# Attention output of some token groups by seven block products for pairs of tiles

## The chip, the cores and the metric

The kernel runs on one core of one Trainium2 chip. The metric is the device time of one execution in microseconds (us). The time before is the median of three runs, 1319.13 us (1318.87 to 1319.29).

## What is computed

Two layers with the same weights, each a linear-attention block followed by a feed-forward block with squared ReLU, on 2048 tokens of width 640 (32 heads of 20), in fp32:

```python
x = A_x
x = x + _A_ref(_layernorm(x), A_wqkv, A_wo)
x = x + _B_ref(_layernorm(x), B_w1, B_b1, B_w2, B_b2)
# the same two lines once more

# _A_ref: q, k, v = x @ wqkv; pq, pk = phi(q), phi(k)
kv = jnp.einsum("bhsd,bhse->bhde", pk, v)
z = jnp.einsum("bhsd->bhd", pk)
num = jnp.einsum("bhqd,bhde->bhqe", pq, kv)
den = jnp.einsum("bhqd,bhd->bhq", pq, z)[..., None] + 1e-6
return (num / den).reshape(B, S, D) @ wo
# _B_ref: h = relu(x @ w1 + b1) ** 2; return h @ w2 + b2      (F = 1728)
```

## The kernel before, in words

**Tiles and exact products.** The 2048 tokens are 16 tiles of 128 rows; four tiles make a group (`TG`, groups 0 to 3). Every fp32 operand of a matmul is split into a high and a low part (`split`: ScalarE copies the rounded high part, VectorE subtracts to get the low part), and each product is three matmuls: high by low, low by high, high by high.

**A layer.** First the attention sums over all tokens are formed. Since kv is the same for all tokens, kv and `wo` are multiplied together once per layer into one 640 by 640 matrix. It is kept split in SBUF as five tiles `M[0]` to `M[4]` of 128 rows (`uM` in the profile). The attention output of a tile is then its normalized pq, transposed, times M: 5 row blocks x 2 column halves of 320 x 3 matmuls = 30 matmuls of 128x320.

**The feed-forward block** runs over the four groups. For each group, `fc1` takes 14 steps c (15 matmuls of 128x512 each, 10 in the last); `act` follows each on ScalarE (Relu, Square) and writes to the tile `R`. Then come 28 steps n of `fc2_step` (12 matmuls of 128x320, or fewer), which already multiply by seven block products with sums and differences formed by `s_op`; `u_hi` (ScalarE) and `u_lo` (VectorE) split them into the five slots of the tile `arena`. The results are added to the residual tile `xr[t]` by `fc2_add`.

**Work beside it.** While group g goes through the feed-forward block, the attention output of the four tiles of group g + 1 is computed (`single`). For a tile t: `b_load_pq` loads pq; `b_den` forms the denominator in a tile `pr`; `b_blocks` divides and transposes 32x32 blocks into a tile `y`; `blocks_move` puts the blocks in place with 16 small ScalarE copies (32x160) into `z`; `p_split` splits into `pTs`; `out` issues the 30 matmuls, in PSUM banks 6 and 7, right after `fc1` steps 4, 7, 10 and 13 (`OUTS`); `add` adds them to `xr[t]` and takes the layernorm's sums; `store` normalizes and writes to DRAM; later `spread_in` and `x_split` bring the tile into `xTb`, the input of the next group's `fc1`.

**Order.** Nothing is scheduled by a tool: each engine runs its instructions in the order in which the code emits them, and `at(g, c, f)` and `on(n, f)` put f after step c of group g (n below zero means the end of the group before, n from 14 on means its `fc2` part, two steps to one). After step c the order is: `fc1` matmuls on TensorE, `load_ring`, `act`, the ("pe", c) events, the other events of c in the order of their registration.

**Weights.** They do not fit in SBUF. `Units` streams them from DRAM copies (`kept`) through a ring of six buffers `u`; a unit's load is issued by SyncE (SP), in order with all other loads and stores, when the matmuls of the unit six places earlier are done. `load_stay` loads the units of `fc2` that stay (`uw`), one per step from c = 3 of group 0. In layer 0, group 0 also runs the last part of the weight preparation (`prep_last`).

Of the kernel before, what the change touches and what calls it, by code (L numbers as in the profile page):

```python
# [13 lines left out]
P = 128  # L14
# [37 lines left out]
AHEAD = 2  # L52
F_BUFS, X_BUFS = 8, 5
OUTS = (4, 7, 10, 13)


def unit_range(k):
# [8 lines left out]
def kernel(  # L66
# [44 lines left out]
    def ftile(name):  # L111
        return tmp.tile([P, D], F32, tag="f", name=name, bufs=F_BUFS)
# [30 lines left out]
    def wtile(name):  # L143
        return tmp.tile([P, 4 * D], R32, tag="w", name=name, bufs=DC)
# [6 lines left out]
    class FirstLoads:  # L151


        def __init__(self):
            self.todo = [(nm, c) for nm in ("k", "q") for c in range(DC)]
            self.pending = []

            self.halves = []
# [46 lines left out]
        return [kq[c][:, :, s] for c in range(DC)]  # L205


    uses = []
    for g in range(NG):
        uses += [(g, "w1", c) for c in range(NF)]  # L210
        uses += [(g, m, k) for m in ORDER for k in range(1, PAIRS)]

    def unit_len(nm, c):
        if nm == "w1":
            return 2 * D if c < 13 else DC * P
        a, b = unit_range(c)
        return 2 * HD * (b - a)
# [7 lines left out]
    for m in ORDER:  # L225
        for k in range(PAIRS):
            a, b = unit_range(k)
            keep((m, k), [P, 2, b - a, HD])

    class Prep:  # L230

# [99 lines left out]
    class Units:  # L331


        def __init__(self, short):
            self.at = {}
            self.ring = list(uses)
            self.moved = (NG - 1, ORDER[-1], 0) if short else None
            if short:
                self.ring.insert(self.ring.index((NG - 1, ORDER[-1], 1)), self.moved)
            self.stay = [(m, 0) for m in ORDER]  # L340
            self.spare = []
            self.free = 0
# [21 lines left out]
                self.at[m, k] = u  # L364

        def used(self, g, nm, c):
            if nm == "w1" or c > 0 or (g, nm, c) == self.moved:
                self.free += 1

        def get(self, g, nm, c):  # L370
            at_ring = nm == "w1" or c > 0 or (g, nm, c) == self.moved
            return self.at[(g, nm, c) if at_ring else (nm, c)]

    sts = {}
# [12 lines left out]
    def ln_apply(t, dst, xt):  # L387
        mv, rs = sts.pop(t)
        nc.vector.tensor_scalar(dst, xt, mv[:, 0:1], rs, op0=ALU.subtract, op1=ALU.mult)
# [51 lines left out]

    def blocks_T(src):
        y = ftile("y")
        nc.vector.transpose(out=y, in_=src)  # L446
        return [y]

# [99 lines left out]
    for layer in range(N_LAYERS):  # L548
# [151 lines left out]

        pq, xr, pT, yzp, yzx, xn = {}, {}, {}, {}, {}, {}
        dens, xTb = {}, {}
        wu = Units(layer < N_LAYERS - 1)

        def b_load_pq(t):
            if t < NT:
# [14 lines left out]

        def b_ops(t):

            pr = ftile("pr")
            nc.vector.tensor_tensor(out=pr, in0=pq[t], in1=zbc, op=ALU.mult)
            yield
            den = small.tile([P, H], F32, tag="den", name="den")
            nc.vector.tensor_reduce(
                den, pr.rearrange("p (h d) -> p h d", d=DH), axis=mybir.AxisListType.X, op=ALU.add
            )  # L730
            dens[t] = den
            yield
            den = dens.pop(t)
            nc.vector.tensor_scalar(den, den, PHI_EPS, None, op0=ALU.add)
            nc.vector.reciprocal(den, den)
            v = pq[t].rearrange("p (h d) -> p h d", d=DH)
            nc.vector.tensor_tensor(
                out=v, in0=v, in1=den[:, :, None].to_broadcast([P, H, DH]), op=ALU.mult
            )
            yield  # L740
            yzp[t] = blocks_T(pq.pop(t))

        b_gen = {}

# [452 lines left out]
        pTs = wtile("pTs").rearrange("p (b j n) -> p b j n", b=2, j=2)  # L1197

        def fc1(g, c):
            ps = bank(c % 4)  # L1200
# [41 lines left out]
        def comb(out, x, y, k, op):  # L1242
            nc.vector.tensor_tensor(out=quad(*out, k), in0=quad(*x, k), in1=quad(*y, k), op=op)  # L1243
# [97 lines left out]
        def at(g, n, f):  # L1341
            events.setdefault((g, n), []).append(f)
# [19 lines left out]
        def single(g, i):  # L1362

            t, b = TG * (g + 1) + i, OUTS[i]

            def on(n, f):
                if n < 0 and g > 0:
                    at(g - 1, NF + N_STEPS + 2 * n, f)
                elif n >= NF:
                    at(g, NF + int(2 * (n - NF)), f)  # L1370
                else:
                    at(g, max(n, 0), f)
# [12 lines left out]

            def out():
                yzp.pop(t)
                for j in range(2):
                    s = slice(j * HD, (j + 1) * HD)
                    ps.append(bank(6 + j)[:, :HD])  # L1390
                    for c in range(DC):
                        a = pT[t][:, :, c * P : (c + 1) * P]
                        mm3(ps[j], a[:, 0], a[:, 1], M[c][:, 0, s], M[c][:, 1, s], c == 0, c == DC - 1)
                pT.pop(t)

            def add():
                for j in range(2):
                    v = xr[t][:, j * HD : (j + 1) * HD]
                    nc.vector.tensor_tensor(out=v, in0=ps[j], in1=v, op=ALU.add)
                ln_stats(("b", t), xr[t])  # L1400

            def store():
                xn[t] = ftile("xn")
                ln_apply(("b", t), xn[t], xr[t])
                xd[t] = spread_out(xn.pop(t))

            at(g, ("pe", b), out)
            on(b + 1 + 0.5 * (i == 3), add)
            on(b + 2, store)
            on(b + 3, lambda: f_bias(t))  # L1410

            def load():
# [4 lines left out]
            steps(lambda: x_split(t), (g, n + 4), (g, n + 5), (g, n + 6))  # L1417

        def ffn_events(g):
            for k in range(PAIRS):  # L1420
# [134 lines left out]
```

## Time and profile before

| | before |
|---|---|
| median of three runs | 1319.13 us |
| the profiled execution's own time | 1318.48 us |
| its span, first to last instruction | 1316.8 us |
| instructions | 20883 |
| HBM read / written | 242.82 MB / 65.54 MB |

The profile is one execution. PE is TensorE's matmuls and PEld its weight loads, DVE is VectorE, ACT ScalarE, POOL GpSimd, SP SyncE, which issues DMAs; L489 is line 489 of the code before. Group rows give the line, the engine, the output and the inputs, the shape and the count, and after the bar the busy time and the mean of one in ns. The matmuls overlap in the pipeline, so the mean of one (309 ns for 128x320) is longer than the distance from one to the next.

### The profile page before, as it was taken

To read this page: it belongs to the slowest core of one execution; us is meant where nothing else is said; L and a number is where in the kernel's file an instruction comes from. 1 tells how busy PE (TensorE), PEld (TensorE's weight loads), DVE (VectorE), ACT (ScalarE), POOL (GpSimd) and SP (SyncE) were. 2 spreads that over 40 slices of the span, in tenths; PEclk is the share of its full clock that TensorE was granted. 3 is DMA by queue.
4 is the path that set the end of the run, shared out by engine and by line. 5 is a ranking of instruction groups with operands and counts; after the bars stand their busy time and mean duration, and the time that the engine had idled before them with its cause. 6 is when DMAs were issued, how large, how long until landed. Compare 5 with 4: busy or idle time off the path is not lost.

```text
span 1316.8 us, 20883 instructions
## 1 busy us (share of the span) xinstructions
PE 1309.1 (99%) x7477; PEld 1192.5 (91%) x7477; DVE 863.6 (66%) x1575; ACT 735.4 (56%) x1594; POOL 218.7 (17%) x289
## 2 busy tenths in 40 slices
PE   9999999999999999999999999999999999999998
PEld 8888889989988988998988899999899899889888
DVE  8888958767944954833856677586576559459045
ACT  5888967785475467334322233487844744754242
POOL 2333310064012002101012122001320120120000
PEclk9999999999999999999999999999999999999999
DMA  6888985699974985898954456554869659749756
GB/s 196 248 277 271 306 248 167 250 355 387 321 287 156 297 303 170 268 359 292 360 165 123 126 146 169 128 199 169 312 216 346 211 190 327 284 147 297 286 188 218
DMA packets 135036, 321.57 MB, mean 244 GB/s; under 512 B 16710, under 2 KB 61894, under 8 KB 134294
## 3 DMA queue, kind: packets, MB, share of 16 engines
q1 hardware_dynamic: 127702, 297.96, 67.7%
q0 software_dynamic: 7232, 22.29, 6.5%
q8 instruction: 59, 0.97, 0.3%
q14 instruction: 43, 0.35, 0.1%
HBM read 242.82 MB, written 65.54 MB: 234 GB/s over the span
## 4 chain that ended last, share of the span: by engine, by line
PE 92%; DVE 3%; ACT 2%; DMA 2%; SPq 1%; issue 0%; POOL 0%; ACTq 0%; DVEq 0%
PE PS L489 33%; PE PS L1214 28%; PE PS L1297 26%; PE PS L516 3%; ACT z L475 1%; PE PS L1050 1%; PE PS L1063 1%; DMA kept<-uprep 1%; DMA st<-in_B_w_dram 1%; PE PS L846 0%; DVE uprep L313 0%; DVE xT L505 0%; DVE bn L379 0%; DVE r L599 0%; PE PS L393 0%
## 5 line engine op out<-in xcount | busy, mean ns | idle before, releaser
L1214 PE MATMUL PS<-xTb,u 128*128 128x512 f32 x1640 | 376.6, 389 | 0.0
L1214 PEld LDWEIGHTS PS<-xTb,u 128*128 128x128 f32 x1640 | 306.8, 188 | 62.5
L489 PE MATMUL PS<-kq,xT 128*128 128x320 f32 (+2 forms) x1575 | 284.3, 334 | 1.4 <-DVE xT L505 1.4
L489 PEld LDWEIGHTS PS<-kq,xT 128*128 128x128 f32 x1575 | 250.3, 188 | 29.1 <-DVE xT L505 2.0
L1297 PE MATMUL PS<-u,arena 128*128 128x320 f32 x1644 | 250.2, 309 | 0.0
L1297 PEld LDWEIGHTS PS<-u,arena 128*128 128x128 f32 x1644 | 243.4, 188 | 0.0
L1278 DVE TENSOR_TENSOR arena<-R,arena 128x512 fp32r<-128x512 f32 (+1 forms) x200 | 140.8, 706 | 134.9 <-ACT arena L1269 134.5
L1269 ACT ACTIVATE arena<-R 128x512 fp32r<-128x512 f32 (+1 forms) x200 | 117.9, 593 | 158.1 <-PE PS L1297 132.0
L455 ACT ACTIVATE z<-y 32x160 f32<-32x160 f32 x512 | 171.1, 334 | 48.6 <-DVE y L446 42.7
L1225 ACT ACTIVATE R<-PS,b1sb 128x512 f32<-128x512 f32 x104 | 71.5, 688 | 128.9 <-PE PS L1214 127.9
L489 PE MATMUL PS<-kh,xh 128*128 128x512 f32 x480 | 124.4, 393 | 0.0
L383 POOL TENSOR_SCALAR rs<-mv 128x1 f32<-128x1 f32 x64 | 34.7, 543 | 513.3 <-DVE mv L381 513.3
L489 PE MATMUL PS<-uM,pTs 128*128 128x320 f32 x720 | 109.4, 309 | 0.0
L489 PEld LDWEIGHTS PS<-uM,pTs 128*128 128x128 f32 x720 | 107.5, 188 | 1.9
L1297 PE MATMUL PS<-uw,arena 128*128 128x320 f32 x660 | 106.1, 309 | 0.0
L489 PEld LDWEIGHTS PS<-kh,xh 128*128 128x128 f32 x480 | 87.3, 188 | 15.3 <-DVE xT L505 0.2
L1297 PEld LDWEIGHTS PS<-uw,arena 128*128 128x128 f32 x660 | 99.2, 188 | 0.4 <-DVE x L1311 0.2
L1243 DVE TENSOR_TENSOR R<-R 128x512 f32<-128x512 f32 (+1 forms) x128 | 79.5, 625 | 26.0 <-ACT R L1226 26.0
L475 ACT ACTIVATE z<-y 32x160 f32<-32x160 f32 x272 | 90.9, 334 | 3.3
L591 ACT ACTIVATE r<-PS 128x512 f32<-128x512 f32 (+1 forms) x64 | 27.7, 434 | 96.4 <-PE PS L489 95.4
L1226 ACT ACTIVATE R<-R 128x512 f32<-128x512 f32 x104 | 65.8, 633 | 3.3
L1311 DVE TENSOR_TENSOR x<-PS,x 128x320 f32<-128x320 f32 x112 | 53.3, 484 | 21.1 <-PE PS L1297 20.3
(135 smaller groups left out, 1281.3 us busy)
## 6 DMA issues: line engine op xcount, KB each, us to landing
u<-kept SPq DMA_DIRECT2D x113, 640.0 KB, 5.4
u<-kept_w SPq DMA_DIRECT2D x104, 640.0 KB, 5.8
u<-kept SPq DMA_DIRECT2D x56, 320.0 KB, 6.1
kept<-uprep SPq DMA_DIRECT2D x49, 320.0 KB, 5.7
z<-xb SPq DMA_DIRECT2D x160, 80.0 KB, 5.4
pqt<-pq SPq DMA_DIRECT2D x32, 320.0 KB, 6.3
acc<-r POOLq DMA_DIRECT2D x28, 320.0 KB, 4.8
uw<-kept SPq DMA_DIRECT2D x14, 640.0 KB, 7.0
```

The source lines that it names most:

```text
L455: nc.scalar.activation(zv[j * B32 : (j + 1) * B32, :, i, :], yv[i * B32 : (i + 1) * B32, :, j, :], AF.Copy)
L475: nc.scalar.activation(zv[j * B32 : (j + 1) * B32, :, i, :], yv[i * B32 : (i + 1) * B32, j], AF.Copy)
L489: nc.tensor.matmul(ps, a, b, start=first and i == 0, stop=last and i == 2)
L516: nc.tensor.matmul(ps[:, j * 512 : j * 512 + HD], aT[:, k, c, :], w[c][:, l, j * HD : (j + 1) * HD], start=c == 0 and (k, l) == (1, 0), st ...
L1214: nc.tensor.matmul(ps, a[:, d, :], bb[:, d, :], start=(d, i) == order[0], stop=(d, i) == order[-1],)
L1225: nc.scalar.activation(r, v, AF.Relu, bias=b1sb[:, c : c + 1])
L1226: nc.scalar.activation(r, r, AF.Square)
L1243: nc.vector.tensor_tensor(out=quad(*out, k), in0=quad(*x, k), in1=quad(*y, k), op=op)
L1269: nc.scalar.activation(u[:, 0], v, AF.Copy)
L1278: nc.vector.tensor_tensor(out=u[:, 1], in0=v, in1=u[:, 0].bitcast(F32), op=ALU.subtract)
L1297: nc.tensor.matmul(ps, x, y, start=opens and k == 0 and p == 0 and e == 0, stop=k == PAIRS - 1 and p == b - a - 1 and e == len(seq) - 1, s ...
L1311: nc.vector.tensor_tensor(out=v, in0=ps, in1=v, op=ALU.add)
```

## The change

In group 3 of layer 0 and groups 2 and 3 of layer 1 the attention output is no longer computed tile by tile (`single`) but for pairs of tiles (`pairs`, `pair`). Rows 0 to 511 of M make a 2x2 block matrix (256 rows x 320 columns each), two tiles make the other (128 tokens x 256 each), and their product is formed by seven block products instead of eight; the last 128 rows of M (`M[4]`, `rest4`) are multiplied as before. A pair takes 7 x 6 + 12 = 54 matmuls instead of 60, at four places after `fc1` steps c0 + 4 to c0 + 7 with c0 = 1 and 6. VectorE forms four sums and differences in place in the moved tiles `z` (`s_op`), and each block is split when it is ready (`hi` on ScalarE, `lo` on VectorE) into one of four slots.

The sums and differences of M are made once per layer by `mix_M`, in group 1 of layer 0 and in group 0 of layer 1: VectorE adds high and low parts (`whole`), GpSimd forms them (`mix`), ScalarE and VectorE split them (`high`, `low`), SP stores them to DRAM (`store`, eight DMAs per layer) and loads one of them over the right half of `M[0]` and `M[1]` (`place`, two DMAs). The other three stream through the ring as units `m6`, `m7`, `m4`, twice per group.

In every tile, `b_den` now writes to a tile `y` that `b_blocks` uses again for the transposed blocks, instead of two tiles.

```diff
+PAIR_AT = (1, 6)
+PQ_AT, DEN_AT, TURN_AT = (-7, -5, -3, -1), (-3.5, -1, 1, 3), (-2.5, 0, 2, 4)
+MOVES_AT = (
+    ((-2, 0), (-1.5, 1), (-1, 2), (-0.5, 3)), ((0, 0), (1, 1), (1, 2), (2, 3)),
+    ((3, 0), (4, 1), (5, 2), (5, 3)), ((6, 0), (6, 1), (7, 2), (7, 3)),
+)
+MIX_G = (1, 0)
...
+                if MIX_G[layer] < g < NG - 1:
+                    for j, c0 in enumerate(PAIR_AT):
+                        if c0 + 5 <= c <= c0 + 7:
+                            uses.append((g, ("m6", "m7", "m4")[c - c0 - 5], j))
...
-            pr = ftile("pr")
+            pr = ftile("y")
...
-            yzp[t] = blocks_T(pq.pop(t))
+            yzp[t] = blocks_T(pq.pop(t), pr)
...
+        def pair(g, j):
...
+            quads = {1: (0, lo2), 5: (1, lo2), 6: (0, lo2), 2: (0, hi2), 7: (1, lo2), 3: (0, hi2), 4: (1, hi2)}
+            order = (1, 5, 6, 2, 7, 3, 4)
+            bk = {1: 4, 6: 4, 7: 4, 4: 4, 5: 5, 3: 5, 2: 6, "d": 7}
...
+            def hi(m):
+                nc.scalar.activation(slot(m)[:, 0], part(m), AF.Copy)
+
+            def lo(m):
+                u = slot(m)
+                nc.vector.tensor_tensor(out=u[:, 1], in0=part(m), in1=u[:, 0].bitcast(F32), op=ALU.subtract)
...
+            def add(m):
+                h, half = adds[m]
+                v = xr[t0 + h][:, half * HD : (half + 1) * HD]
+                nc.vector.tensor_tensor(out=v, in0=bank(bk[m])[:, :HD], in1=v, op=ALU.add)
+
+            on(c0 + 1, begin)
+            for n, ops in (
+                (2, ((lo, 1), (s_op, 1), (hi, 5))),
+                (3, ((lo, 5), (s_op, 2), (hi, 6), (hi, 2))),
+                (4, ((lo, 6), (lo, 2), (s_op, 3), (s_op, 4), (hi, 7), (hi, 3))),
+                (5, ((lo, 7), (lo, 3), (hi, 4))),
+                (6, ((lo, 4),)),
+            ):
+                for f, m in ops:
+                    on(c0 + n, lambda f=f, m=m: f(m))
+            on(c0 + 2, rest_hi)
+            on(c0 + 3, rest_lo)
+            plan = ((1, 5, "d"), (6, 2), (7, 3), (4,))
+            for i, ms in enumerate(plan):
+                for m in ms:
+                    at(g, ("pe", c0 + 4 + i), lambda m=m: product(m))
...
+        def mix_M(g):
+            first = (g * N_STEPS + 2) % SLOTS * 4 * HT + 2 * HT
+            v = arena.rearrange("p s j k n -> p (s j k n)")[:, first : first + 4 * D]
...
+            def high(p):
+                for u, x in parts(p):
+                    nc.scalar.activation(u[:, 0], x, AF.Copy)
...
+            for c, f, p in (
+                (0, whole, 0), (0, mix, 0), (2, high, 0), (3, low, 0), (3, store, 0), (3, whole, 1),
+                (3, mix, 1), (5, high, 1), (6, low, 1), (6, store, 1),
+            ) if g else (
+                (1, whole, 0), (1, mix, 0), (2, whole, 1), (2, mix, 1), (3, high, 0), (4, low, 0), (4, store, 0),
+                (5, high, 1), (6, low, 1), (6, store, 1),
+            ):
+                at(g, c, lambda f=f, p=p: f(p))
+            for p in range(2):
+                at(g, NF + 4 + 4 * p, lambda p=p: place(p))
...
+        mix_M(MIX_G[layer])
         for g in range(NG):
             ffn_events(g)
         for g in range(NG - 1):
+            if g > MIX_G[layer]:
+                pairs(g)
+                continue
             for i in range(TG):
                 single(g, i)
```

More of the change, by code (lines that the diff above doesn't have):

```diff
@@ L205, in wk, with uses_of @@
         return [kq[c][:, :, s] for c in range(DC)]
[L208 to L211, printed above, removed]
+    def uses_of(layer):
+        uses = []
+        for g in range(NG):
+            for c in range(NF):
+                uses.append((g, "w1", c))
+                if MIX_G[layer] < g < NG - 1:
+                    for j, c0 in enumerate(PAIR_AT):
+                        if c0 + 5 <= c <= c0 + 7:
+                            uses.append((g, ("m6", "m7", "m4")[c - c0 - 5], j))
+            uses += [(g, m, k) for m in ORDER for k in range(1, PAIRS)]
+        return uses
     def unit_len(nm, c):
+        if nm in ("m4", "m6", "m7"):
+            return 2 * D
         if nm == "w1":
@@ L228 @@
             keep((m, k), [P, 2, b - a, HD])
+    for m in ("m4", "m5", "m6", "m7"):
+        kept[m, 1] = keep((m, 0), [P, 2, 2, HD])
     class Prep:
@@ L331, with __init__ @@
     class Units:
-        def __init__(self, short):
+        def __init__(self, uses, short):
             self.at = {}
-            self.ring = list(uses)
+            self.ring = uses
             self.moved = (NG - 1, ORDER[-1], 0) if short else None
@@ L366, in used @@
         def used(self, g, nm, c):
-            if nm == "w1" or c > 0 or (g, nm, c) == self.moved:
+            if isinstance(nm, str) or c > 0 or (g, nm, c) == self.moved:
                 self.free += 1
         def get(self, g, nm, c):
-            at_ring = nm == "w1" or c > 0 or (g, nm, c) == self.moved
+            at_ring = isinstance(nm, str) or c > 0 or (g, nm, c) == self.moved
             return self.at[(g, nm, c) if at_ring else (nm, c)]
@@ L440, in turn, with blocks_T @@
         return y
-    def blocks_T(src):
-        y = ftile("y")
+    def blocks_T(src, y=None):
+        if y is None:
+            y = ftile("y")
         nc.vector.transpose(out=y, in_=src)
@@ L702 @@
         dens, xTb = {}, {}
-        wu = Units(layer < N_LAYERS - 1)
+        wu = Units(uses_of(layer), layer < N_LAYERS - 1)
         def b_load_pq(t):
@@ L1196 @@
         arena = tmp.tile([P, SLOTS, 2, 2, HT], R32, tag="T", name="arena", bufs=2)
-        pTs = wtile("pTs").rearrange("p (b j n) -> p b j n", b=2, j=2)
+        wt = wtile("pTs")
+        pTs = wt.rearrange("p (b j n) -> p b j n", b=2, j=2)
         def fc1(g, c):
@@ L1364, in single @@
             t, b = TG * (g + 1) + i, OUTS[i]
[L1366 to L1372, printed above, removed]
+            on = after(g)
             if t > TG:
@@ L1400, in add, with after, on, norm_out @@
                 ln_stats(("b", t), xr[t])
[L1402 to L1405, printed above, removed]
             at(g, ("pe", b), out)
             on(b + 1 + 0.5 * (i == 3), add)
-            on(b + 2, store)
+            on(b + 2, lambda: norm_out(t))
             on(b + 3, lambda: f_bias(t))
+            x_in(g, i)
+        def after(g):
+            def on(n, f):
+                if n < 0 and g > 0:
+                    at(g - 1, NF + N_STEPS + 2 * n, f)
+                elif n >= NF:
+                    at(g, NF + int(2 * (n - NF)), f)
+                else:
+                    at(g, max(n, 0), f)
+            return on
+        def norm_out(t):
+            xn[t] = ftile("xn")
+            ln_apply(("b", t), xn[t], xr[t])
+            xd[t] = spread_out(xn.pop(t))
+        def x_in(g, i):
+            t = TG * (g + 1) + i
             def load():
@@ new lines, in pairs @@
+        def pairs(g):
+            on = after(g)
+            both = [pair(g, j) for j in range(2)]
+            for p in both:
+                next(p)
+            for i, moves in enumerate(MOVES_AT):
+                t = TG * (g + 1) + i
+                on(PQ_AT[i], lambda t=t: b_load_pq(t))
+                on(DEN_AT[i], lambda t=t: b_den(t))
+                on(TURN_AT[i], lambda t=t: b_blocks(t))
+                for n, q in moves:
+                    on(n, lambda t=t, q=q: blocks_move(yzp[t], (q,)))
+                on(PAIR_AT[i // 2] + 1, lambda t=t: b_load_x(t))
+                x_in(g, i)
+            for p in both:
+                next(p, None)
@@ new lines, in mix_M, with whole, mix, parts @@
+        def mix_M(g):
+            first = (g * N_STEPS + 2) % SLOTS * 4 * HT + 2 * HT
+            v = arena.rearrange("p s j k n -> p (s j k n)")[:, first : first + 4 * D]
+            h = [R[:, i, 1].rearrange("p c n -> p (c n)")[:, HT + D * j : HT + D * (j + 1)] for i in range(2) for j in range(2)]
+            a, b, q = (h[0], h[3]), (h[1], h[0]), (h[2], h[1])
+            if g == 0:
+                x1 = x1_odd["tile"]
+                b, q = (h[1], x1[:, 2]), (h[2], x1[:, 3])
+            oq = v[:, : 2 * D].rearrange("p (j m n) -> p j m n", j=2, m=2)
+            o6, o4 = (v[:, D * i : D * (i + 1)].rearrange("p (j n) -> p j n", j=2) for i in (2, 3))
+            lo, hi = slice(0, HD), slice(HD, D)
+            def whole(p):
+                for out, m in ((a[p], p), (b[p], 2 + p)):
+                    nc.vector.tensor_tensor(
+                        out=out, in0=M[m][:, 0].bitcast(F32), in1=M[m][:, 1].bitcast(F32), op=ALU.add
+                    )
+            def mix(p):
+                for out, x, y, op in (
+                    (q[p][:, lo], a[p][:, hi], a[p][:, lo], ALU.subtract),
+                    (q[p][:, hi], b[p][:, hi], a[p][:, hi], ALU.subtract),
+                    (a[p][:, hi], q[p][:, hi], a[p][:, lo], ALU.add),
+                    (b[p][:, lo], b[p][:, lo], a[p][:, hi], ALU.subtract),
+                ):
+                    nc.gpsimd.tensor_tensor(out=out, in0=x, in1=y, op=op)
+            def parts(p):
+                return (
+                    (oq, q[p].rearrange("p (m n) -> p m n", m=2)), (o6, a[p][:, hi]), (o4, b[p][:, lo]),
+                )
+            def high(p):
+                for u, x in parts(p):
+                    nc.scalar.activation(u[:, 0], x, AF.Copy)
+            def low(p):
+                for u, x in parts(p):
+                    nc.vector.tensor_tensor(out=u[:, 1], in0=x, in1=u[:, 0].bitcast(F32), op=ALU.subtract)
+            def store(p):
+                for i, m in enumerate(("m5", "m7")):
+                    nc.sync.dma_start(kept[m, 0][:, :, p], oq[:, :, i].bitcast(F32))
+                nc.sync.dma_start(kept["m6", 0][:, :, p], o6.bitcast(F32))
+                nc.sync.dma_start(kept["m4", 0][:, :, p], o4.bitcast(F32))
+            def place(p):
+                nc.sync.dma_start(M[p][:, :, HD:].bitcast(F32), kept["m5", 0][:, :, p])
+            for c, f, p in (
[4 more added lines that the diff above has]
+                (5, high, 1), (6, low, 1), (6, store, 1),
+            ):
+                at(g, c, lambda f=f, p=p: f(p))
+            for p in range(2):
+                at(g, NF + 4 + 4 * p, lambda p=p: place(p))
```

75 lines of the change are left out of this document (added).

## The prediction

> **What bounds the kernel now.** I read the page's busy table and granted clock first, then busy time by stage, then the groups by line, then the timeline around the new waits.
>
> ```profile
> PE 1309.1 (99%) x7477; PEld 1192.5 (91%) x7477; DVE 863.6 (66%) x1575; ACT 735.4 (56%) x1594; POOL 218.7 (17%) x289
> PEclk9999999999999999999999999999999999999999
> L489 PE MATMUL PS<-uM,pTs 128*128 128x320 f32 x720 | 109.4, 309 | 0.0
> 574.04 46.65 PE L1214 MATMUL PS<-xTb,u 128*128 128x512 f32 x205
> core 0: us, PE busy (x) PEld busy (x) DVE busy (x) ACT busy (x) POOL busy (x), PEclk, DMA share, GB/s
> 467.65:531.80 64.15, 64.15 (x328) 56.07 (x327) 29.93 (x55) 43.99 (x100) 10.38 (x12) 1.00 0.67 233
> 574.04:620.53 46.49, 46.49 (x208) 38.49 (x206) 10.23 (x21) 19.58 (x31) 5.28 (x13) 1.00 0.92 338
> 905.04:969.19 64.15, 64.15 (x328) 56.07 (x326) 35.32 (x63) 44.42 (x101) 16.83 (x18) 1.00 0.75 266
> 1075.58:1117.82 42.24, 42.24 (x291) 42.24 (x290) 38.00 (x67) 15.70 (x28) 3.32 (x5) 1.00 0.93 290
> ```
>
> TensorE is busy for 99% of the span, at the full clock in every slice, and the 720 matmuls of the attention output had no idle time before them. The windows are fc1 of group 2 in layer 0 (with the output of group 3 beside it), fc1 of group 3 (with none), fc1 of group 0 in layer 1, and an fc2 stage. In each, PE is busy for the whole stretch: its queue sets the time, and the others follow with room. A matmul that goes is worth its distance to the next, if nothing new makes PE wait.
>
> **The sum on PE.** fc1 without attention work takes 46.49 us for 205 matmuls, 0.2268 each, so 3.40 per step of 15. With four tiles it takes 64.15: 17.66 for 120 matmuls of 128x320, 0.1472 each. Two pairs need 108, 12 fewer: 1.77 us per group, 5.30 for the three groups. Seams between 512 and 320 columns: an fc2 stage, 288 matmuls of 320 without seams, takes 42.24, 0.1467 each. The 0.0005 more, over 120, is 0.06 us for eight seams; pairs have sixteen, at most 0.07 us more per group. Sum: 5.30 - 0.2 = 5.1 us. The bounds are 5.30 (seams free) and nothing below this sum as long as PE doesn't wait.
>
> **Conversions in the pair groups.** Durations come from the nearest shapes:
>
> ```profile
> L455 ACT ACTIVATE z<-y 32x160 f32<-32x160 f32 x512 | 171.1, 334 | 48.6 <-DVE y L446 42.7
> L1225 ACT ACTIVATE R<-PS,b1sb 128x512 f32<-128x512 f32 x104 | 71.5, 688 | 128.9 <-PE PS L1214 127.9
> L1226 ACT ACTIVATE R<-R 128x512 f32<-128x512 f32 x104 | 65.8, 633 | 3.3
> L1269 ACT ACTIVATE arena<-R 128x512 fp32r<-128x512 f32 x168 | 105.5, 628 | 149.0 <-PE PS L1297 124.5 <-DVE R L1243 22.4 <-DVE x L1311 1.1
> L1269 ACT ACTIVATE arena<-R 128x256 fp32r<-128x256 f32 x32 | 13.1, 410 | 9.1 <-PE PS L1297 7.6 <-DVE R L1243 1.5
> L591 ACT ACTIVATE r<-PS 128x128 f32<-128x128 f32 x19 | 5.2, 273 | 15.6 <-PE PS L489 15.6
> L1278 DVE TENSOR_TENSOR arena<-R,arena 128x512 fp32r<-128x512 f32 x168 | 125.6, 751 | 116.3 <-ACT arena L1269 115.9
> L1278 DVE TENSOR_TENSOR arena<-R,arena 128x256 fp32r<-128x256 f32 x32 | 15.1, 472 | 18.6 <-ACT arena L1269 18.6
> L1243 DVE TENSOR_TENSOR R<-R 128x512 f32<-128x512 f32 x96 | 65.5, 682 | 26.0 <-ACT R L1226 26.0
> L1243 DVE TENSOR_TENSOR R<-R 128x256 f32<-128x256 f32 x32 | 14.6, 456 | 0.0
> L599 DVE SCALAR_TENSOR_TENSOR r<-PS,r 128x128 f32<-128x128 f32 x19 | 5.5, 292 | 3.0 <-ACT rq L591 2.9
> L1399 DVE TENSOR_TENSOR x<-PS,x 128x320 f32<-128x320 f32 x48 | 22.1, 484 | 17.3 <-PE PS L489 17.3
> L1325 ACT ACTIVATE pTs<-z 128x640 fp32r<-128x640 f32 x24 | 17.4, 723 | 0.0
> L1327 DVE TENSOR_TENSOR pTs<-z,pTs 128x640 fp32r<-128x640 f32 x24 | 18.9, 787 | 9.0 <-ACT pTs L1325 9.0
> L379 DVE BATCH_NORM_STATS2 bn<-x 128x6 f32<-128x320 f32 x64 | 28.1, 481 | 0.3
> L381 DVE BATCH_NORM_AGGREGATE mv<-bn 128x2 f32<-128x12 f32 x64 | 13.4, 209 | 2.2
> L389 DVE TENSOR_SCALAR xn<-x,mv,rs 128x640 f32<-128x640 f32 x32 | 19.4, 605 | 8.5 <-POOL rs L384 8.5
> ```
>
> A pair adds 7 x 0.41 + 2 x 0.27 = 3.4 us on ACT and 7 x 0.47 + 2 x 0.29 + 4 x 0.46 + 8 x 0.48 = 9.6 on DVE; it drops two splits (1.4 and 1.6) and four adds (1.9 on DVE). For a group that is ACT 44.0 + 4.0 = 48.0 and DVE 29.9 + 12.2 = 42.1 of 62.4 us: room on average, so what counts is when each block is ready. I walk the second pair, the fuller one, from the group's first matmul. fc1 step 7 ends at 8 x 3.40 + 30 x 0.147 = 31.6. Behind it ACT does act (1.32), a 512-column split (0.63), hi 1 (0.41) and the last tile's eight moves (2.7): 36.7. Step 8 ends at 37.2: act, a split, hi 5, the two rest parts: 40.1. DVE meanwhile does a split, lo 1, a sum, the first pair's last add (its product ends at 38.5), one apply (0.61) and one tile's statistics (2 x 0.48 + 0.21): 40.8; then a split (0.75), an fc2 sum (0.68), lo 5, a sum and the two rest parts: 43.7. PE comes to product 1 at 11 x 3.40 + 54 x 0.147 = 45.4 and needs lo 5 at 46.3, the rest parts at 47.2. Ready 3.5 us early. The later blocks have a step of 3.40 plus a product place (2.2) for one link of ACT and DVE, 2 to 3 us with what stands before them. So the conversions cost nothing; their cover is fc1, and gone it costs PE one to one. Moves in parts of four are the same sixteen copies, spread, and one f buffer less per tile loosens the rotation: nothing.
>
> **Loads.** Each pair group loads six more units of 640 KB, 3.9 MB in all, on a stage of 64.15 us at 233 GB/s (15 MB): a DMA share of 0.67 becomes about 0.85.
>
> ```profile
> u<-kept SPq DMA_DIRECT2D x113, 640.0 KB, 5.4
> kept<-uprep SPq DMA_DIRECT2D x49, 320.0 KB, 5.7
> kept_kq<-kq SPq DMA_DIRECT2D x10, 640.0 KB, 9.2
> ```
>
> The shortest lead in the ring is that of the unit of fc1 step 9: issued when step 6 is done (7 x 3.40 + 2.2 = 26.0), used at 38.5, 12.5 us against 5.4 to land. Free. The two `place` loads per layer fall into fc2, some 45 us ahead of their use.
>
> **mix_M.** This is the one place where new waits stand in engine queues that were tight. In layer 1 its steps fall into fc1 of group 0, which starts at 905.04:
>
> ```profile
> 918.70 0.82 DVE L1327 TENSOR_TENSOR pTs<-z,pTs 128x640 fp32r<-128x640 f32 x1 [2.03 <-ACT pTs L1325]
> 922.07 4.56 PE L489 MATMUL PS<-uM,pTs 128*128 128x320 f32 x30
> 925.93 2.75 ACT L455 ACTIVATE z<-y 32x160 f32<-32x160 f32 x8
> 930.73 0.83 DVE L1327 TENSOR_TENSOR pTs<-z,pTs 128x640 fp32r<-128x640 f32 x1 [2.53 <-ACT pTs L1325]
> 933.80 2.77 ACT L455 ACTIVATE z<-y 32x160 f32<-32x160 f32 x8 [1.87 <-DVE y L446]
> 936.69 4.56 PE L489 MATMUL PS<-uM,pTs 128*128 128x320 f32 x30
> 945.63 0.77 DVE L1327 TENSOR_TENSOR pTs<-z,pTs 128x640 fp32r<-128x640 f32 x1
> 951.31 4.56 PE L489 MATMUL PS<-uM,pTs 128*128 128x320 f32 x30
> ```
>
> `high(0)` enters ACT's queue at 925.93. No row has its 320-column parts; I take 0.45, between 0.41 (256) and 0.63 (512), so 0.72 + 2 x 0.45 = 1.6 us for the three, the bounds being 1.5 and 2.0. The next split, 930.73, comes 1.6 us later and ends at 933.2, ahead of 936.69. `low(0)` follows the first part from 926.65 on, 0.79 + 2 x 0.53 on DVE, ends at 928.5, and the four stores go out by then. `high(1)` writes to the same arena halves, so on ACT it waits for them to land: 928.5 + 5.7 = 934.2, and ends at 935.8. Behind it stand the moves that before began at 933.80: 2.0 us late. ACT has no pause from there to the next tile's split, whose low half shifts from 945.63 to 947.6 and ends at 948.4, ahead of the product at 951.31. It holds with 2.9 us, until the stores take 8.6 us to land. Layer 0's group 1 starts `mix_M` a step earlier. SP waits for `low` before the stores, and ring units queue behind them; these have six steps. Cost: nothing, in a range of 0 to 2.8 us (the stores at twice 5.7).
>
> The sixteen GpSimd sums between them read what VectorE reads:
>
> ```profile
> L269 POOL TENSOR_TENSOR wq<-wb,wa 128x320 f32<-128x320 f32 x5 | 5.6, 1121 | 0.0
> L269 POOL TENSOR_TENSOR wq<-wa 128x320 f32<-128x320 f32 x5 | 4.3, 870 | 0.0
> ```
>
> One such sum is at times 0.25 us longer than another; no row shows DVE held for a whole one. Four in a row take 3.5 to 4.5 us; I take 3.7, one long and three short.
>
> **The rivals.**
> A. The stores land late in layer 1's group 0, and PE waits before a product. For it: DMA share 0.75 there already, and a store row of 9.2 us. At 9.2 PE waits 0.6 us; at 11.4, 2.8. Between 1314.6 and 1316.8 us.
> B. GpSimd's sums hold VectorE. In the same place four of them, 3.7 us, fall on the stretch in which DVE splits the first tile (918.70 to 919.5, its product at 922.07) and divides the second. Held for all of it, the split would end at 923.2, and PE waits 1.1 us; the later shifts hide behind that wait. 1315.1 us. Against it: the 0.25 above. The Trainium skill (SBUF — State Buffer, Who interferes with whom) says that a VectorE instruction with two SBUF inputs and a GpSimd instruction that reads SBUF lock each other out, the second to issue waiting for the whole of the first; by that rule B is the forecast.
> C. Slower: the links between ACT and DVE are longer than one step, so that PE waits in all six pairs at its first products. It decides from 3.5 + 0.85 = 4.4 us of lateness in each pair (5.1 / 6 = 0.85 us eats the gain). If the last tile's sixteen moves (5.5 us) stood ahead of the first block instead of beside it, each pair waits 2.0 us: 12 us, 1326 us. For it: ACT would be busy 77% of the stage and its queue is strict. Against it: the walk.
> D. A load of the ring is late by 2 us or so in each pair group: about 1319, no change. The lead of 12.5 us speaks against it.
>
> **How the numbers follow.** The profiled execution took 1318.48 us, of which its span is 1316.8; the median of the runs is 1319.13, 0.65 higher. Less 5.1: 1313.4 by the profiled one, 1314.0 by the median, which I predict. Chances: forecast 0.58, A 0.14, B 0.08, C 0.14, D 0.06. A measurement tells 0.2%, 2.6 us, from no change: faster means below 1316.5. That holds for the forecast, B and nearly all of A: 0.79; slower for C and a little of D, 0.15; between, 0.06. The forecast's own range is 1313.2 to 1314.6; to leave out no more than two in ten I go from 1313.1 to 1318.
>
> **What would show it.** PE busy falls by 5.1 us and the span with it; each of the three fc1 stages is 62.4 us, the other fc1 and fc2 stages as before; 684 matmuls read `pTs`, with idle time before none of them. Idle PE before those of the new line, released by DVE, would mean C; before a product in layer 1's group 0, with ACT waiting for a DMA out of `arena`, A; long DVE instructions beside GpSimd's, B; PE waiting for a load of `u`, D. The prediction is wrong if fc1 of the pair groups is not shorter than 63.5 us.

## The result and the profile after

After the change the kernel takes 1314.82 us (median of 8 runs, 1313.54 to 1317.01), the kernel before 1318.60 us (8 runs, 1318.25 to 1319.29): a ratio of 0.9972, 95% interval 0.9962 to 0.9981. It is 3.8 us faster, and the interval lies below 1. The forecast was 1314.0 us. The runs after lie 3.5 us apart, those before 1.0.

The profiled execution took 1314.40 us, its span is 1312.7. From its page, the busy table and the clock:

```profile
PE 1305.7 (99%) x7441; PEld 1188.5 (91%) x7441; DVE 920.8 (70%) x1685; ACT 745.9 (57%) x1648; POOL 237.4 (18%) x305
PEclk9999999999999999999999999999999999999999
```

PE lost 36 matmuls and 3.4 us of busy time; DVE gained 57 us. Busy time by stage (the columns as in the prediction): fc1 of group 2 and of group 3 in layer 0, fc1 of group 0 in layer 1 (where M is mixed), then fc2 of groups 1 and 2 in layer 1:

```profile
468.19:530.66 62.47, 62.47 (x315) 54.31 (x314) 37.93 (x79) 43.97 (x107) 7.61 (x10) 1.00 0.76 273
573.00:619.49 46.49, 46.49 (x207) 38.50 (x206) 10.23 (x21) 19.57 (x31) 5.26 (x13) 1.00 0.91 337
904.39:968.54 64.15, 64.15 (x327) 56.08 (x326) 46.03 (x72) 46.77 (x107) 26.79 (x26) 1.00 0.84 306
1073.25:1115.62 42.37, 42.37 (x290) 42.24 (x289) 41.20 (x72) 16.80 (x33) 6.02 (x7) 1.00 0.99 324
1178.09:1220.47 42.38, 42.38 (x291) 42.25 (x290) 37.11 (x66) 15.01 (x27) 6.01 (x7) 1.00 0.98 317
```

A pair group's fc1 went from 64.15 to 62.47 us; the other fc1 stages are what they were. The two fc2 stages shown, which lie behind pair groups, went from 42.24 to 42.37 and 42.38, and their DMA share from 0.93 and 0.90 to 0.99 and 0.98. The groups of the attention output, x360 by tiles and x324 by pairs, 684 in all, with no idle time recorded before them:

```profile
L508 PE MATMUL PS<-uM,pTs 128*128 128x320 f32 x360 | 54.7, 309 | 0.0
L1528 PE MATMUL PS<-uM,pTs 128*128 128x320 f32 x216 | 35.6, 309 | 0.0
L1528 PE MATMUL PS<-u,pTs 128*128 128x320 f32 x108 | 18.7, 308 | 0.0
```

**Where the time went.** Idle times this short are taken from the starts of successive matmuls in the traces. What a distance exceeds its usual value by (147 ns for 320 columns, 227 for 512, 120 for 256, 110 for 128) is a gap. "FFN" sums the gaps over 15 ns ahead of matmuls that read `xTb`, `arena` or `pTs`, "elsewhere" the rest (the start and the attention sums), "rest" is the span less both and less what lies before the first and behind the last matmul's start. The labels below `after` are the experiments.

```
             time     span   elsewhere  FFN    rest
before      1318.48  1316.76   15.85    0.21  1295.30
after       1314.40  1312.67   16.80    0.55  1290.26
mix_only    1318.76  1317.06   16.16    0.21  1295.29
again       1313.93  1312.23   16.35    0.62  1290.22
late_bias   1314.32  1312.62   17.19    0.20  1290.17
one_mix     1316.75  1315.05   17.01    2.75  1290.26
late_place  1315.31  1313.60   17.70    0.62  1290.22
both        1315.39  1313.70   16.74    1.68  1290.24
both_pq     1313.18  1311.48   16.06    0.20  1290.18
eased       1314.81  1313.09   16.58    1.21  1290.26
single_loads 1318.61 1316.90  16.02    0.55  1295.28
more_loads  1317.60  1315.88   17.37    3.09  1290.27
more_hold   1320.85  1319.15   16.24    7.71  1290.17
slow_conv   1338.86  1337.13   16.41   25.43  1290.27
```

The rest is 5.0 to 5.1 us less in every kernel with pairs: the matmuls' own gain, whole. In the profiled execution 0.95 us more went elsewhere and 0.34 in gaps of the feed-forward block; 0.36 less lies behind the last matmul's start. Of the 0.95 us, 0.52 lie in the first 60 us, ahead of the first instruction that the change alters, and 0.41 in layer 1's attention sums (800 to 910 us). The gaps of the first 60 us alone differ by 1.2 us between these executions (4.64 to 5.84).

### The profile page after: what moved, and what is told of

It is laid out like the page before. It is cut to its first block, busy times and chain, and to the rows that moved or that the text cites. A ratio compares the mean times of both kernels' runs of the same rounds, so it can differ in the third digit from the quotient of the medians.

```text
span 1312.7 us, 21122 instructions
## 1 busy us (share of the span) xinstructions
PE 1305.7 (99%) x7441; PEld 1188.5 (91%) x7441; DVE 920.8 (70%) x1685; ACT 745.9 (57%) x1648; POOL 237.4 (18%) x305
## 4 chain that ended last, share of the span: by engine, by line
PE 93%; DVE 2%; ACT 2%; DMA 1%; issue 0%; SPq 0%; POOL 0%; ACTq 0%; DVEq 0%; POOLq 0%
PE PS L508 30%; PE PS L1234 28%; PE PS L1317 26%; PE PS L1528 4%; PE PS L535 3%; ACT z L494 1%; PE PS L1069 1%; PE PS L1082 1%; DMA st<-in_B_w_dram 1%; PE PS L865 0%; PE PS L656 0%; DMA kept<-uprep 0%; DVE xT L524 0%; DVE uprep L331 0%; DVE r L618 0%
## 5 line engine op out<-in xcount | busy, mean ns | idle before, releaser
L1298 DVE TENSOR_TENSOR arena<-R,arena 128x512 fp32r<-128x512 f32 (+1 forms) x200 | 135.2, 682 | 83.0 <-ACT arena L1289 82.6
L1263 DVE TENSOR_TENSOR R<-R 128x512 f32<-128x512 f32 (+1 forms) x128 | 88.5, 694 | 14.8 <-ACT R L1246 14.8
L617 DVE TENSOR_SCALAR r<-r 128x512 f32<-128x512 f32 (+1 forms) x64 | 21.3, 332 | 69.7 <-ACT r L610 69.6
L1331 DVE TENSOR_TENSOR x<-PS,x 128x320 f32<-128x320 f32 x112 | 53.0, 484 | 19.2 <-PE PS L1317 18.4
L1539 DVE TENSOR_TENSOR x<-PS,x 128x320 f32<-128x320 f32 x48 | 23.2, 489 | 45.5 <-PE PS L1528 44.9
```

Of the source, the lines that this page charges most:

```text
L1331: nc.vector.tensor_tensor(out=v, in0=ps, in1=v, op=ALU.add)
```

## The experiments

All are run beside the kernel before, whose medians were 1318.81 to 1318.86 us. Edits are to the changed kernel.

| kernel | median, us | lowest to highest (runs) | ratio to before, 95% |
|---|---|---|---|
| again | 1314.50 | 1313.93 to 1315.05 (5) | 0.9953 to 0.9978 |
| late_bias | 1314.32 | 1314.06 to 1314.94 (5) | 0.9951 to 0.9978 |
| more_hold | 1321.99 | 1320.85 to 1325.68 (7) | 1.0015 to 1.0036 |
| one_mix | 1315.22 | 1314.15 to 1316.75 (8) | 0.9961 to 0.9982 |
| mix_only | 1319.13 | 1318.51 to 1320.06 (11) | 0.9994 to 1.0012 |
| late_place | 1313.84 | 1313.48 to 1315.31 (5) | 0.9949 to 0.9977 |
| both | 1314.36 | 1313.63 to 1315.39 (5) | 0.9954 to 0.9979 |
| both_pq | 1313.56 | 1313.18 to 1315.30 (5) | 0.9951 to 0.9976 |
| eased | 1314.73 | 1313.48 to 1314.99 (5) | 0.9954 to 0.9979 |
| more_loads | 1317.09 | 1313.51 to 1319.15 (9) | 0.9970 to 0.9990 |
| single_loads | 1319.32 | 1318.21 to 1321.02 (11) | 0.9995 to 1.0013 |
| slow_conv | 1338.02 | 1336.15 to 1343.03 (4) | 1.0132 to 1.0168 |

### VectorE behind a pair group

The timeline of the kernel after, in fc2 of group 1 of layer 1 (start and duration in us):

```profile
1079.57 3.59 POOL L1214 TENSOR_TENSOR x<-x,b2bc 128x640 f32<-128x640 f32 x2
1079.61 2.10 DVE L1263 TENSOR_TENSOR R<-R 128x512 f32<-128x512 f32 x1
1081.64 1.80 DVE L1298 TENSOR_TENSOR arena<-R,arena 128x256 fp32r<-128x256 f32 x1
...
1098.83 0.65 DVE L1298 TENSOR_TENSOR arena<-R,arena 128x512 fp32r<-128x512 f32 x1
1099.40 0.84 PE L1317 MATMUL PS<-u,arena 128*128 128x320 f32 x4
```

`f_bias` of the second pair's two tiles runs twice in a row on GpSimd, and the two VectorE instructions that start beside it take 2.10 and 1.80 us instead of 0.68 and 0.42. Both end 0.3 to 0.6 us after the GpSimd sum beside them. VectorE then has no pause left, and at 1099.40 PE starts on an operand whose split ends only at 1099.48: there and in a second place of the stage PE loses 0.04 to 0.09 us each.

`again` is the changed kernel once more:

> The changed kernel, unaltered, for its spread and a second profile. All theories: a median of 1314.0 to 1315.5 us. Theory F (the three fc2 stages behind the pair groups have lost VectorE's lead, so that whatever comes late there goes through to PE): executions differ by up to 3 us, and in the second profile the matmuls out of arena in those three stages have gaps of 0.1 us or more. Theory M (the mixing of M in layer 1's group 0 is what varies): the gaps stand before the last products of that group. Theory S (the start varies): they stand in the first 40 us.

It took 1314.50 us, and its FFN gaps stand in the same three stages (0.12, 0.14, 0.14 us). Its five runs lie 1.1 us apart, not the 3 that theory F gave and not the 3.5 of the first eight: a spread from so few runs proves little, here and below. `late_bias`:

```diff
-                on(c0 + 9, lambda h=h: f_bias(t0 + h))
+                if j:
+                    at(g + 1, 1 + 2 * h, lambda h=h: f_bias(t0 + h))
+                else:
+                    on(c0 + 9, lambda h=h: f_bias(t0 + h))
```

> The bias sums of the second pair's two tiles move from the first fc2 steps behind a pair group to steps 1 and 3 of the next group's fc1. Theory F: VectorE is no longer held for 2.5 us at the start of those fc2 stages, the gaps of 0.36 us in all before matmuls out of arena go, and the time is 0.4 to 1 us below the changed kernel's, 1313.8 to 1314.4 us, with executions within about 1 us of each other. Theories M and S: the gaps go, at most 0.4 us, and the spread of 3 us stays.

The gaps are gone (FFN 0.20, what the kernel before has). The median, 1314.32, is 0.2 us lower, which these runs cannot tell from nothing. But the sums did not move to the next fc1. GpSimd ran them right behind its instruction before them, a MEMSET at 1101.34, and that is in the same fc2 stage, 22 us later and again two in a row:

```profile
1101.73 3.45 POOL L1214 TENSOR_TENSOR x<-x,b2bc 128x640 f32<-128x640 f32 x2
```

So the run shows that the two sums cost PE nothing at that place, not that they are out of fc2. In the three kernels below that have this edit they run there too. `more_hold`:

```diff
             for h in range(2):
                 on(c0 + 9, lambda h=h: f_bias(t0 + h))
+            if j:
+                on(c0 + 9, lambda: nc.gpsimd.tensor_tensor(
+                    out=xr[t0], in0=xr[t0], in1=b2bc, op=ALU.subtract))
+                on(c0 + 9, lambda: f_bias(t0))
```

> Two more GpSimd sums (b2 subtracted and added again) behind the second pair's two, so four instead of two in a row at the start of the three fc2 stages. Theory F: VectorE is held for about 2.5 us more in each, nothing is left to hide it, and PE waits about 2.5 us in each: 7 to 8 us slower than the changed kernel, 1322 us. Rival (VectorE has room in fc2, as the prediction took for granted): the same time, 1314.8 us. Rival that GpSimd does not hold VectorE: the same time, and no VectorE instruction over 1.2 us beside the new sums.

1321.99 us, as theory F expected. Its timeline and PE's waits:

```profile
1087.55 1.64 DVE L1298 TENSOR_TENSOR arena<-R,arena 128x512 fp32r<-128x512 f32 x1
1089.24 0.99 PE L1317 MATMUL PS<-uw,arena 128*128 128x320 f32 x5 [1.08 <-DVE arena L1298]
...
PE PS L1317 <- DVE arena L1298: 3.2, 3, 1.1
```

The gaps of the three stages sum to 2.46, 2.50 and 2.49 us. So GpSimd's sums do hold VectorE, and behind a pair group nothing hides it.

### Mixing M

`one_mix` leaves the mixing out in layer 1:

```diff
-                at(g, c, lambda f=f, p=p: f(p))
+                if layer == 0:
+                    at(g, c, lambda f=f, p=p: f(p))
```

> The mixing of M is left out in layer 1, which uses the mixed blocks of layer 0. Theory M: layer 1's group 0 has no late stores or splits any more, the spread goes down to about 1 us and the median by 0.5 us or more, to 1314.2 us or below. Theory F: median and spread stay, 1314.8 us; the slack before the last products of that group rises from 0.66 to about 4.4 us, as before the change.

Median 1315.22, and 2.6 us between its eight runs: theory M (1314.2 or below, about 1 us) falls. `mix_only` makes and stores the blocks and uses none:

```diff
-                if MIX_G[layer] < g < NG - 1:
+                if NG < g < NG - 1:
...
-            for p in range(2):
-                at(g, NF + 4 + 4 * p, lambda p=p: place(p))
...
-            if g > MIX_G[layer]:
+            if g > NG:
```

> The changed kernel with single instead of pairs in all groups: the mixing of M is made and stored, and neither loaded over M nor used. The output stays the reference's. Prediction (mixing costs nothing): the kernel before, 1318.6 to 1319.1 us. Rival A (late stores, late splits): up to 2.8 us more, 1321 us. The slack before layer 1's group 0's last product is then 0.66 us or less, as in the changed kernel.

1319.13 us against 1318.81: no cost that these 11 and 15 runs can tell (-0.06% to +0.12%). It was near, though. The third and the fourth tile of group 0 in the changed kernel, split on VectorE and product on PE:

```profile
948.75 0.77 DVE L1347 TENSOR_TENSOR pTs<-z,pTs 128x640 fp32r<-128x640 f32 x1
950.66 4.56 PE L508 MATMUL PS<-uM,pTs 128*128 128x320 f32 x30
...
962.86 0.77 DVE L1347 TENSOR_TENSOR pTs<-z,pTs 128x640 fp32r<-128x640 f32 x1
964.14 2.06 PE L508 MATMUL PS<-uM,pTs 128*128 128x320 f32 x13
```

The split ends 1.1 us ahead of the third product and 0.5 ahead of the fourth (0.66 ahead of the first matmul that reads it).

### The spread, and the transfers in fc2

The profiled execution of `one_mix`, 1316.75 us, has its 2.1 us of gaps in fc2 of group 0 in layer 1. The window, PE's waits there, and the loads of that stretch with their time to land; the second fence has the same window and loads of the kernel after:

```profile
968.80:1013.00 44.20, 42.80 (x289) 42.10 (x288) 38.02 (x67) 16.77 (x32) 3.33 (x5) 1.00 0.95 290
...
PE PS L1317 <- DMA u<-kept: 1.4, 2, 1.0
...
u<-kept SPq DMA_DIRECT2D x5, 320.0 KB, 8.4
z<-xb SPq DMA_DIRECT2D x12, 80.0 KB, 8.4
```

```profile
968.54:1010.78 42.24, 42.24 (x290) 42.24 (x289) 40.22 (x71) 19.18 (x38) 4.00 (x6) 1.00 0.93 318
...
u<-kept SPq DMA_DIRECT2D x5, 320.0 KB, 7.0
z<-xb SPq DMA_DIRECT2D x12, 80.0 KB, 6.7
```

The same transfers took 1.4 to 1.7 us longer to land, and PE waited for units of the ring. The amount alone does not explain it: the stage moved 290 GB/s here, 318 in the kernel after, which lost nothing in it, and 288 in the kernel before. `late_place` moves the two `place` loads out of that stage:

```diff
-                at(g, NF + 4 + 4 * p, lambda p=p: place(p))
+                at(g + 1, 0, lambda p=p: place(p))
```

> The two place loads per layer move from fc2 of the mixing group (steps 4 and 8) to step 0 of the next group's fc1, where the pair group runs and has 17 us until it reads them. Theory R (the run-to-run spread of 3 us comes from that fc2 stage, where PE waited up to 2.1 us for late units of the ring while the DMA engines were 95% busy, and the place loads are what filled them): units land at least 3 us ahead of use there, executions lie within about 1 us, median 1314.2 us; the 0.36 us of gaps behind the pair groups stay. Rival R2 (the ring is short there for other reasons: two more pq loads, or SP): spread and median as the changed kernel, 1314.8 us. Rival R3 (the loads are now late for the first pair's product 5): PE waits before it, 1315 us or more.

Median 1313.84, no wait before product 5 (R3 falls), but runs up to 1315.31: the spread stays, so `place` is not the whole of it. That slowest run is the profiled one, and no ring unit is late in it: its FFN gaps are 0.62 us, as in `again`, and it lost 17.70 us elsewhere, the most of all. `both` (this and `late_bias`):

> Late place loads and late bias sums together. Theories R and F: no gaps behind the pair groups and no late units, 1313.6 to 1314.1 us, within 1 us of each other. R2: the median of the late bias sums alone, 1314.3 us.

1314.36, a miss. Its profiled execution, 1315.39 us, waited in another fc2 stage, that of group 2 in layer 1; the window and PE's waits in it:

```profile
1178.70:1222.40 43.70, 43.02 (x289) 42.31 (x288) 35.77 (x66) 15.34 (x27) 5.88 (x7) 1.00 1.01 310
...
PE PS L1317 <- DMA u<-kept: 0.4, 1, 0.4
PE PS L1317 <- DVE arena L1298: 0.3, 1, 0.3
```

The second wait is not for a unit: it stands behind the moved bias sums, which run from 1207.51 to 1210.96 in this trace. No mixing and no `pq` load falls into the stage. In the kernel before the same stage had:

```profile
1181.96:1224.20 42.24, 42.24 (x290) 42.24 (x289) 34.18 (x61) 15.78 (x27) 3.32 (x5) 1.00 0.90 281
```

281 GB/s became 310 to 317, 11.86 MB became 13.42 in the kernel after: there two stores of `xn`, 16 loads of `z` and six small units are issued in this stage, before one, 12 and five (1.0 of the 1.6 MB), and the DMA engines have next to no time left. Two more edits are meant to ease it:

```diff
-PQ_AT, DEN_AT, TURN_AT = (-7, -5, -3, -1), (-3.5, -1, 1, 3), (-2.5, 0, 2, 4)
+PQ_AT, DEN_AT, TURN_AT = (-6.5, -4, -2, 0), (-3.5, -1, 1, 3), (-2.5, 0, 2, 4)
```

> Besides, the four pq loads of a pair group come later, (-6.5, -4, -2, 0) for (-7, -5, -3, -1), so that one of them falls into fc1. R2: the ring gets its room only here, 1313.6 us and a spread of 1 us, against 1314.3 us with the two other edits. Theory R: the same as with the two other edits, within 0.3 us.

For `eased`, also:

```diff
-                on(c0 + 7 + h, lambda h=h: norm_out(t0 + h))
+                on(c0 + 6 + h, lambda h=h: norm_out(t0 + h))
```

> Late place loads, late bias sums, late pq loads, and a pair's tiles are normalized and stored one step earlier, so that their way through DRAM starts 3.4 us earlier. Theories R and F: nothing is left of either cost, 1313.2 to 1313.8 us, within 1.5 us of each other. Rival (the DMA engines fill fc2 whatever the order): 1313.5 to 1314.5 us with a spread of 2 us.

1313.56 and 1314.73 us: `both_pq` has the lowest median, but the two lie in each other's range, and 5 runs of each settle nothing. Nor does `eased` test the transfers cleanly. The gaps of its profiled execution (1.0 us in the two fc2 stages of layer 1) are waits for VectorE, beside the bias sums at their new place:

```profile
1206.91 3.45 POOL L1214 TENSOR_TENSOR x<-x,b2bc 128x640 f32<-128x640 f32 x2
1209.79 1.72 DVE L1298 TENSOR_TENSOR arena<-R,arena 128x512 fp32r<-128x512 f32 x2
1210.96 0.71 PE L1317 MATMUL PS<-u,arena 128*128 128x320 f32 x3 [0.25 <-DVE arena L1298]
```

The rival, that the DMA engines fill fc2 whatever the order, stays: it had 1313.5 to 1314.5, which 1314.73 misses by less than the 1313.2 to 1313.8 of theories R and F. It was then tested by a dose, `more_loads`, and by the same dose where the engines had time left, `single_loads` (on `mix_only`):

```diff
+            for p in range(2):
+                at(g + 1, NF + 6 + 6 * p, lambda p=p: place(p))
+                if layer:
+                    at(g + 2, NF + 6 + 6 * p, lambda p=p: place(p))
```

> The two place loads are issued a second time, with the same data, at steps 6 and 12 of the three fc2 stages behind pair groups: 0.64 MB more in each, some 2 us of what the DMA engines move there. Theory R (these stages have no room left in the DMA engines, so that ring units come late): 1 to 2 us more per stage, 1317 to 1320 us, with PE waiting for loads of u. Rival (the DMA engines still have room): 1314.8 us.

> The same six extra loads in the kernel with single in all groups and the mixing made (they overwrite half of M[0] and M[1], so that later groups compute something else). Theory R: before the change these stages had 7 to 10% of the DMA time free, which takes most of 2 us in 42: at most 1 us slower than without the loads, 1319.1 to 1320.2 us, a smaller rise than with pairs. Rival (a load costs the same wherever it falls): the same rise as with pairs.

With pairs 1317.09, 2.3 to 2.6 us more than the changed kernel's two medians, spread over 5.6 us; without pairs 1319.32 against 1319.13. PE's waits in the profiled execution of `more_loads`:

```profile
PE PS L1234 <- DMA u<-kept_w: 1.0, 1, 1.0
PE PS L1317 <- DMA u<-kept: 0.5, 3, 0.2
PE PS L508 <- DMA kq<-kept_kq: 0.5, 1, 0.5
```

The same 2 MB cost about 2.4 us in the one median and 0.2 in the other, which speaks for theory R. It is not settled by it: in the profiled execution 1.7 us of the gaps lie in layer 0 at the end of group 1's fc2 and in the first step behind it, ahead of the first added load, and behind the added loads late units cost 0.8 us, in one stage of three, where theory R had 1 to 2 us in each.

### The conversions' lead

`slow_conv` puts a known delay on ScalarE in front of each pair's blocks:

```diff
-                hi(1)
+                for _ in range(17):
+                    hi(1)
```

> The first block of each pair is copied 17 times instead of once, 16 x 0.41 = 6.6 us more on ScalarE ahead of all other blocks. Prediction (conversions hidden, the blocks ready 3.5 us early by its walk, 4.1 to 4.9 by the trace after): PE waits 1.7 to 3.1 us in each of six pairs, 10 to 19 us in all, 1325 to 1334 us. Rival C (no lead): 6.6 us in each, 1354 us. Rival that PE never waits for them: 1314.8 us.

1338.02 us: 23 us more, 3.9 per pair, above the 1.7 to 3.1 expected and far from rival C's 6.6. The delay itself was larger than the 6.6 us expected. The seventeen copies of one pair, in a row on ScalarE:

```profile
1058.15 7.60 ACT L1474 ACTIVATE pTs<-z 128x256 fp32r<-128x256 f32 x17
```

That is 7.2 us more than one copy (0.40), in each pair. The first pair of group 2 in layer 0 waits 1.78 us before its second product and 0.56 behind that product's first matmul, 2.33 in all, as its lead of 4.85 us has it (7.2 - 4.85 = 2.35). All waits in the six pairs come to 18.5 us in the profiled execution. What comes on top shows in two neighbouring windows about the second pair of layer 1's group 1:

```profile
1066.60:1069.50 2.90, 0.15 (x1) 0.00 (x1) 0.94 (x3) 2.79 (x8) 0.00 (x0) 0.91 0.61 175
1069.50:1075.60 6.10, 5.32 (x17) 4.80 (x18) 6.07 (x17) 5.53 (x14) 3.52 (x5) 0.50 0.25 100
```

After the wait the granted clock is 0.50 for some 6 us, and matmuls of 320 columns stand 267 ns apart instead of 147. With two shorter stretches of this kind it costs 5.7 us. The larger delay and this part are why the expectation was too low.

## Why the prediction was right, point by point

- **The sum on PE** (5.1 us): right. 5.0 to 5.1 in every kernel with pairs (column "rest"), 1.68 per fc1 stage against 1.70 forecast.
- **Conversions cost nothing, ready 3.5 us early**: right. In the trace after, the second pair's block 5 ends 4.1 us ahead of its product and the rest parts 4.2; the first pair has 4.85. The tightest block is another, the second pair's block 6, with 3.1 us: its low half, usually 0.42 us, takes 3.8 beside the first pair's two bias sums (the first of the two in this row):

```profile
1055.04 4.16 DVE L1478 TENSOR_TENSOR pTs<-z,pTs 128x256 fp32r<-128x256 f32 x2
1055.46 3.11 POOL L1214 TENSOR_TENSOR x<-x,b2bc 128x640 f32<-128x640 f32 x2
```

  The walk counted 2 to 3 us for a link of the later blocks, with 5.6 us to do it in, and had no such hold in it; the room was enough all the same. `slow_conv` used the lead up and made PE wait. Rival C is refuted.
- **Mixing costs nothing**: right in the time (`mix_only`, `one_mix`), too generous in the place. I took the third product of group 0 as the tight one, with 2.9 us; it has 1.3, and the fourth, which I did not walk, 0.66. Rival A was not paid in any profiled execution: 64.15 us for that stage.
- **GpSimd holds VectorE (rival B)**: the step that failed is "no row shows DVE held for a whole one". The trace of before shows it; these are its rows, beside the same bias sum:

```profile
1079.96 2.68 DVE L1278 TENSOR_TENSOR arena<-R,arena 128x512 fp32r<-128x512 f32 x1 [0.54 <-ACT arena L1269]
1080.49 1.59 POOL L1195 TENSOR_TENSOR x<-x,b2bc 128x640 f32<-128x640 f32 x1
```

  2.68 us where the mean was 0.75. I had read the group's mean alone. That VectorE waits for the whole of such a sum agrees with the Trainium skill (SBUF — State Buffer, Who interferes with whom), by which the second of two such instructions to issue waits for the whole of the first. The recorded starts do not show that order in every row: in the kernel after VectorE's start at 1079.61 is 0.04 us the later one, in this row of before it is 0.53 us the earlier, and VectorE waits in both. The price fell elsewhere than rival B had it: not in the mixing but in the bias sums, 0.36 us, which the change puts two in a row.
- **Loads cost nothing**: right for fc1, not shown for fc2, and the main omission. Rival D asked whether a unit is late in fc1, where there is room (share 0.76). I gave fc2 no sum of its own, and there the share rose to 0.98 and 0.99. The two profiled executions of the changed kernel have no wait for a unit; among its variants, the dose aside, PE lost up to 2.1 us to late units (`one_mix`). So such waits can be a part of the spread of 3.5 us, but no trace of the changed kernel shows one. The dose points to the room being gone, and none of four edits brought the spread down for sure.
- **The time**: 0.8 us under the measured 1314.82, and that is in part luck. The kernel before measured 1318.60 beside it, 0.53 less than the 1319.13 that the forecast starts from; the gain is 3.8 us, 1.3 short of the 5.1. Nor did PE's busy time fall by the 5.1 us that I named as the sign: it fell by 3.4, and the gain shows in the distances between matmuls (column "rest"). What the sum of 5.05 leaves out are 0.36 us in the bias sums, waits for transfers that differ from run to run, and 0.2 to 1.8 us "elsewhere" (16.06 to 17.70 in eleven kernels with pairs, 15.85 to 16.16 in three without), in code whose order the change leaves alone. The part of it in the first 60 us runs ahead of the change. In layer 1's attention sums six of the eleven kernels with pairs lost 0.4 to 0.6 us more than the kernel before, the other five and the two further ones without pairs at most 0.1: whether the change has a part in that stays open.

## What to carry over

A kernel that is bound by TensorE for 99% of its span can still pay for what it moves: beside the stage that gets shorter, add up DMA and VectorE for the next one, which inherits the work that no longer fits. Read single long instructions, not only a group's mean, before saying that one engine does not hold another. And look in the trace where a moved instruction really ran: the order of the code fixes its place on its own engine's queue, not the stage of another engine that it falls beside.

## What the hardware showed

- A VectorE instruction that reads a single tile in SBUF was held too, in the kernel after, group 0 of layer 1 (usually 0.17 us):

```profile
932.94 1.78 POOL L1214 TENSOR_TENSOR x<-x,b2bc 128x640 f32<-128x640 f32 x1
933.20 1.56 DVE L753 TENSOR_SCALAR den<-den 128x32 f32<-128x32 f32 x1
```

  Sums with an operand in PSUM (0.49 us), reductions (0.82) and transposes of blocks (0.84) that started beside GpSimd's sums kept their usual times.
- A wait of 2.9 us on PE was followed by some 6 us at half the granted clock, which cost a further 2.6 us. Waits of 1.78 and 0.56 us close together were followed by 3.4 us at half the clock in group 2 of both layers, and by none in group 1 of layer 1 (`slow_conv`, the first pair of group 2 in layer 0 and of group 1 in layer 1):

```profile
492.15:495.56 3.41, 3.41 (x12) 3.12 (x12) 3.31 (x10) 3.29 (x9) 0.00 (x0) 0.50 0.00 0
1042.41:1045.80 3.39, 3.39 (x18) 3.01 (x19) 3.29 (x9) 3.27 (x9) 0.00 (x0) 1.00 0.00 2
```

- The three kernels without pairs agree in "rest" within 0.02 us and the eleven with pairs within 0.1: what differs between executions is waits, ahead of matmuls or behind the last one, and in `slow_conv` the clock.
